# Resorting two turns of a fused linear-attention and SSM kernel: where projections, loads and scans stand

## Chip, core and metric

The kernel runs on one core of one Trainium2 chip. The metric is device time in microseconds (us), a median of runs. The core has a matrix engine (TensorE, PE, whose weight loads are listed apart as PEld), a vector engine (VectorE, DVE), an activation engine (ScalarE, ACT), a general engine (GpSimd, POOL) and a queue engine (SyncE, SP) that issues DMAs. Each engine works through its own list of instructions in order, and waits on semaphores for the others. The order of these lists is written by hand in this kernel, so the place of a call in the Python code is the place of its instructions on every engine.

## What is computed

Gated linear attention over 4 batches, 8 heads, 768 positions and 48 channels, then an SSM block over the heads laid side by side (384 channels):

```python
for t in range(S):                      # attention
    state = alpha[:, :, t, :, None] * state + einsum('bhd,bhde', k[:, :, t], v[:, :, t])
    y[:, :, t] = einsum('bhd,bhde->bhe', q[:, :, t], state)
x = y.transpose(0, 2, 1, 3).reshape(B, S, H * D)
proj = x @ w_in                         # 384 -> 2 * 512
val, gate = proj[..., :512], proj[..., 512:]
for t in range(S):                      # SSM
    h = exp(A_log)[0] * h + val[:, t]
    ys[:, t] = h
out = (silu(gate) * ys) @ w_out         # 512 -> 384
```

All data is float32. The inputs q, k, v and alpha have the shape (4, 8, 768, 48).

## The kernel before

The sequence is cut into 12 groups of 256 positions (`N`), three for each batch, and each group into two chunks of 128. The attention of a group is done by chunks, with running products of alpha, and the SSM of a group follows one turn later. In turn `n` of the main loop (L1012) the kernel does the SSM of group `n`, the attention of group `m = n + 1`, and the running products of group `n + 2`. The diff touches turns 1 to 3, the second to the fourth of the twelve when group 0's SSM ahead of the loop is counted as the first. They have code of their own (n < 3 at L1028, n == 3 at L1069); from turn 4 on the turns are alike.

The pieces of a turn, with the lines that the profile names:

- `products(m)` (L656) is a generator that works on DVE alone but for one check on ACT (`check_alpha`, L631). Its seven steps are: (1) turn alpha by a transposition (L660), put start values in place (L671, L672); (2) the forward scan of products (L674); (3) the ratio and reciprocal (L681 or L683, L687) and the reverse scan of inverse products (L695); (4) turn k into the tile Z (L660); (5) multiply it by the inverse products (L704); (6) turn q into Z (L660); (7) multiply it by the products (L704). `go(count)` lets it do that many steps; a `go` with more than is left does what is left.
- `keys(m, c)` (L717 on PE, L718 on ACT) turns k's half of Z into position-major form.
- `scores(m, c)` (L727) multiplies keys and queries. `masks` makes the result causal: the near half on DVE (L754), the far half by a copy on ACT (L742) and a multiplication on POOL (L743). `masks_apart`, used from turn 3 on, does both halves by ACT (L749) and POOL (L750).
- `state` (L786, L789), `values` (L765) and `carried` (L776) give the attention's output y in PSUM.
- `join(m, engines)` (L791) copies y to SBUF on ACT (L795, L796) and moves it by eight small DMAs (L812) into xT, the SSM's input, with channels on partitions; two heads go by ACT directly (L802). `engines[s]` issues the four moves of the half `s` of the heads.
- `block(n, cc)` (L845) is one quarter of the projection: `project` (L827) multiplies the value half and the gate half, each three matmuls of 256 columns, which the profile shows as six records; `hidden` (L835) is the SSM's scan on DVE; `gate` is Silu on ACT (L842) and a multiplication into the tile f on POOL (L843). `output(n)` (L856, L864, L865) multiplies f by w_out, and stores the result.

`mm` hands out three PSUM banks in a ring, one to each half of a block, to each `keys` and to each half of an output. A half can start once the engine that read the bank's previous tenant is done: DVE's scan for a value half, ACT's Silu for a gate half.

Loads go through SP. `loads(m)` issues alpha, k and q of a group (four DMAs each), `load_v` two for v. `ahead()` (L1022) issues `loads(n + 3)` and `load_v(n + 2)`. Up to eight of SP's DMAs are under way: each issue waits until the eighth before it has landed.

Of the kernel before, what the change touches and what calls it, by code (L numbers as in the profile page):

```python
# [351 lines left out]
def fast(  # L352
# [21 lines left out]
    nc = tc.nc  # L374
# [32 lines left out]
    def pair_of(*dims, dtype=FP32, which=None):  # L407
        if next(next_pair) if which is None else which:
            return [end_ps.tile([C, *dims], dtype, tag=f"b{b}", name="pair") for b in (4, 5)]
        t = both()  # L410
        n = dims[0] * dims[1]
        return [t[:, i, 0:n].rearrange("p (x y) -> p x y", x=dims[0]).bitcast(dtype) for i in range(2)]
# [8 lines left out]
    def load_raw(name, m, engines):  # L421


        b, g = divmod(m, NG)
        src = {"a": alpha, "q": q, "k": k}[name]
        t = raw_bufs[m % NR][name]
        n = 0
        for i in range(2):
            for odd in range(2):
                engines[n % len(engines)].dma_start(  # L430
                    out=t[ds(64 * i + 32 * odd, 32), :, 0:NT * D - 32 * odd],
                    in_=src[b, i::2, ds(g * GC, GC), :]
                    .rearrange("h (c j) d -> c h (j d)", c=32)[:, :, 32 * odd:])
                n += 1
# [16 lines left out]
    def load_v(m, engine, cs=range(G)):  # L451
        b, g = divmod(m, NG)
        for c in cs:
            engine.dma_start(out=vs[m % NV][:, c, :, 0:D],
                             in_=v[b, :, ds(g * GC + c * C, C), :].rearrange("h p d -> p h d"))
# [151 lines left out]
    def natural_qk(m, name, c, tp):  # L607

        if m not in Zs:
            Zs[m] = p2.tile([C, 4, 2, GC], FP32, tag="Z", name="Z")  # L610
        turned(name, m, c, tp)

        def times():
            i, by = {"k": (1, invs), "q": (0, prods)}[name]
            cols = ds(c * C, C)
            if m < 1:
                by = (inv_c[c][:, 1:] if name == "k" else prod_c[c]).rearrange("p (h n) -> p h n", h=4)
            else:
                by = by[:, :, cols]
            nc.vector.tensor_mul(Zs[m][:, :, i, cols], tp, by)  # L620
        return times
# [89 lines left out]
    def keys(m, c, b=None):  # L711

        if (m % NG) * G + c == NG * G - 1:
            return
        tp = mm(4, C, b=b)
        for p in range(4):
            nc.tensor.transpose(tp[:, p, :], Zs[m][:, p, 1, ds(c * C, C)], ident)  # L717
        nc.scalar.activation(ktms[c].rearrange("p a i d -> p a (i d)"), tp, AF.Copy)  # L718
# [11 lines left out]
    def masks(m, c, near_first=False):  # L730
        if near_first:
            masks_near(m, c)
        masks_far(m, c)
        if not near_first:
            masks_near(m, c)
# [55 lines left out]
    def join(m, engines, later=False):  # L791

        y = ys.pop(m)
        y_sb = p2.tile([C, 4, GC], FP32, tag="y_sb", name="y_sb")
        nc.scalar.activation(y_sb[:, 1::2], y[1], AF.Copy)  # L795
        nc.scalar.activation(y_sb[:, 2], y[0][:, 1], AF.Copy)  # L796
        xT = xTs[m] = p2.tile([C, NK, GC], FP32, tag="xT", name="xT")

        def in_place():
            for h in (0, 4):  # L800
                kk, row = divmod(h * D, C)
                nc.scalar.activation(xT[ds(row, D), kk], y[0][ds(16 * h, D), 0], AF.Copy)  # L802

        if not later:
            in_place()
        for h in (1, 5, 3, 7, 2, 6):
            s, a = divmod(h, 4)
            d = 0
            while d < D:
                kk, row = divmod(h * D + d, C)  # L810
                size = min(D - d, C - row)
                engines[s].dma_start(out=xT[ds(row, size), kk], in_=y_sb[ds(64 * s + d, size), a])  # L812
                d += size
        return in_place
# [5 lines left out]
    def project(n, cc):  # L820
        if cc == 0:
            fs[n] = end_sb.tile([C, NI, GC], FP32, tag="f", name="f")
        xT = xTs[n]
        pv, pg = mm(GC), mm(GC)
        for vg, pj in enumerate((pv, pg)):
            for kk in range(NK):
                nc.tensor.matmul(pj, w_in[cc][vg][:, kk, :], xT[:, kk, :],  # L827
                                 start=(kk == 0), stop=(kk == NK - 1))
        return pv, pg
# [3 lines left out]
    def hidden(n, cc, pv):  # L833
        hh = p2.tile([C, GC], FP32, tag=f"h{cc}", name="hh")
        nc.vector.tensor_tensor_scan(  # L835
            out=hh, data0=a_dec[:, cc:cc + 1].to_broadcast([C, GC]), data1=pv,
            initial=prev_h[cc][:, GC - 1:GC] if n % NG else 0.0, op0=ALU.mult, op1=ALU.add)
        prev_h[cc] = hhs[n, cc] = hh

    def gate(n, cc, pg):  # L840
        sg = p2.tile([C, GC], FP32, tag="sg", name="sg")
        nc.scalar.activation(sg, pg, AF.Silu)  # L842
        return lambda: nc.gpsimd.tensor_mul(fs[n][:, cc, :], sg, hhs.pop((n, cc)))  # L843

    def block(n, cc):  # L845
        pv, pg = project(n, cc)
        hidden(n, cc, pv)
        gate(n, cc, pg)()
# [24 lines left out]
    SP, ACT = nc.sync, nc.scalar  # L873

    def loads(m):
        for name in "akq":
            load_raw(name, m, [SP])
# [134 lines left out]
    for n in range(1, N):  # L1012
        m = n + 1
        att = m < N
        steps = products(n + 2) if n + 2 < N else iter(())

        def go(count):
            for _ in range(count):
                next(steps, None)


        def ahead():  # L1022
            if n + 3 < N:
                loads(n + 3)
            if n + 2 < N:
                load_v(n + 2, SP)

        if n < 3:  # L1028
            if n == 1:
                block(n, 0)  # L1030
                for times in [natural_qk(m, name, c, tp) for c in range(G)
                              for name, tp in zip("kq", pair_of(4, C))]:
                    times()
                block(n, 1)
            ahead()
            for c in range(G):
                keys(m, c)
            for c in range(G):
                scores(m, c)
            go(1)  # L1040
            for c in range(G):
                masks(m, c)
            if n == 2:
                block(n, 0)
                go(1)
                block(n, 1)
                go(1)
            else:
                block(n, 2)
                go(1)  # L1050
            state(m, 0)
            values(m, 0)
            values(m, 1)
            state(m, 1)
            carried(m, 0)
            carried(m, 1)
            join(m, (nc.gpsimd, nc.gpsimd) if m == 2 else (SP, SP))
            if n == 2:
                go(2)
                block(n, 2)  # L1060
            go(1)
            block(n, 3)
            go(10)
            output(n)()
            continue

        if n == 3:  # L1069
            for c in range(G):  # L1070
                scores(m, c, 1 - c)
                masks_apart(m, c)
            for c in range(G):
                keys(m, c)
            ahead()
            go(4)
        else:
            state(n, 0)
            values(n, 0)
            values(n, 1)  # L1080
            state(n, 1)
            carried(n, 0)
            carried(n, 1)
            in_place = join(n, (SP, nc.gpsimd), later=True)
            if att:
                scores(m, 0, 1)
                masks_apart(m, 0)
                in_place()
                scores(m, 1, sc=[mm(4, C, b=b) for b in "01"])
                masks_apart(m, 1)  # L1090
                keys(m, 0, "6")
                keys(m, 1, "4")
            else:
                in_place()
            next_mm = itertools.cycle("160")
            ahead()
            go(4)
            output(n - 1, "50")()
        for cc in range(NI):
            block(n, cc)  # L1100
            go(1)
            if cc == 0 and n == N - 1:
                next(end, None)
            if cc == 2 and n > 3:
                for _ in itertools.islice(checks, 2):
                    pass
        if n == N - 2:
            end = check_end()
            next(end)
# [61 lines left out]
```

## Time and profile before

| what | value |
|---|---|
| median of 3 runs | 291.07 us (291.03 to 291.84) |
| the profiled execution | 291.08 us, of which the span from the first to the last instruction is 289.3 us |
| granted TensorE clock | 1.000 |
| DMA | 42.08 MB in 70734 packets, 47508 of them under 512 bytes |
| turns 4 to 10 | about 21.9 us each, from one first projection to the next on PE (118.77, 140.68, 162.61, ...) |
| turns 1, 2, 3 on PE | turn 1 from 47.18 to 70.87, turn 2 to 93.90, turn 3 to 107.27, where turn 4 begins |

A line of the page's list gives an engine's busy time, its share of the span and its instructions. A line of the timeline gives start and length in us, engine, source line, operation, output and inputs, shape and count; in brackets stands how long the engine was idle before it, and what released it. Matmuls overlap in PE's pipeline and their ends are modelled, so that a length is a little more than the time until the next start. In the view of one tile, a line gives the shortest, median and longest duration in ns, and the first and last start in us. "To landing" is the time from a DMA's issue to its last byte.

### The profile page before, as it was taken

Reading aid. Unit: us, or ns where it says so; the run is one execution under the profiler, and the core shown is the slowest. Engines: PE = TensorE matmul, PEld = TensorE weight load, DVE = VectorE, ACT = ScalarE, POOL = GpSimd, SP = SyncE. Lnnn points to the kernel's source line nnn. Section 1 sums busy time; section 2 is a strip of 40 time slices with the busy share of each in tenths; the row PEclk is TensorE's granted clock in tenths of the full one; section 3 lists DMA queues with packets and bytes.
Section 4 is the critical chain, followed back from the end, with each engine's and each line's share of the span. In section 5 each row is a group of like instructions: output and inputs, shape, how many; then the busy total and the mean of one; then the engine's idle time right before and its main releaser. Section 6 shows DMA issues by size and latency. Waiting matters only on the chain. (4 is left out here: it accounts for less than half of the span.)

```text
span 289.3 us, 6236 instructions
## 1 busy us (share of the span) xinstructions
PE 279.4 (97%) x2353; PEld 227.2 (79%) x2353; DVE 211.2 (73%) x263; ACT 109.1 (38%) x242; POOL 139.2 (48%) x165
## 2 busy tenths in 40 slices
PE   7699999999999999999999999999999999999985
PEld 6478877885886988788788788788788788687874
DVE  5998896999999999399599599599589580131221
ACT  2447634432441626316316415416416415313110
POOL 7147792375532765526725725625734734633130
PEclk9999999999999999999999999999999999999999
DMA  9999969999997992992991991991892400201101
GB/s 130 163 162 299 376 129 185 173 250 211 231 220 106 221 200 53 215 205 54 228 189 43 217 204 42 206 212 48 191 198 77 113 2 25 73 0 30 69 5 61
DMA packets 70734, 42.08 MB, mean 145 GB/s; under 512 B 47508, under 2 KB 69656, under 8 KB 70696
## 3 DMA queue, kind: packets, MB, share of 16 engines
q1 hardware_dynamic: 68240, 39.78, 69.8%
q0 software_dynamic: 1408, 1.62, 2.3%
q8 instruction: 20, 0.33, 0.5%
q10 hardware_dynamic: 1048, 0.20, 0.4%
q14 instruction: 18, 0.15, 0.2%
HBM read 33.33 MB, written 4.72 MB: 131 GB/s over the span
## 5 line engine op out<-in xcount | busy, mean ns | idle before, releaser
L827 PE MATMUL mm<-xT,w_in 128*128 128x256 f32 x576 | 127.7, 380 | 0.3 <-ACT A L742 0.3
L827 PEld LDWEIGHTS mm<-xT,w_in 128*128 128x128 f32 x576 | 108.7, 190 | 17.7 <-issue 0.6
L843 POOL TENSOR_TENSOR f<-sg,hh 128x256 f32<-128x256 f32 x48 | 40.4, 843 | 87.2 <-ACT sg L842 61.8
L835 DVE TENSOR_TENSOR_SCAN hh<-a_dec,hh,mm 128x256 f32<-128x256 f32 x32 | 23.7, 741 | 49.6 <-PE mm L827 44.9
L856 PE MATMUL mm<-w_out,f 128*128 128x384 f32 x176 | 59.4, 489 | 0.1
L842 ACT ACTIVATE sg<-mm 128x256 f32<-128x256 f32 x48 | 18.5, 385 | 98.7 <-PE mm L827 96.6
L750 POOL TENSOR_TENSOR A<-A,mask 128x512 f32<-128x512 f32 x32 | 47.7, 1519 | 5.5 <-ACT A L749 5.4
L856 PEld LDWEIGHTS mm<-w_out,f 128*128 128x128 f32 x176 | 32.5, 190 | 21.4 <-POOL f L843 1.0
L812 POOL DMA_DIRECT2D xT<-y_sb x44 | 22.7, 521 | 28.4 <-ACT y_sb L796 26.8
L674 DVE TENSOR_TENSOR_SCAN prod<-aT,first 128x1024 f32<-128x1024 f32 x10 | 23.4, 2340 | 0.3
L695 DVE TENSOR_TENSOR_SCAN inv<-aT,last 128x1025 f32<-128x1025 f32 x10 | 22.9, 2294 | 0.3
L765 PE MATMUL pair<-A,v 128*64 128x128 f32 x352 | 21.3, 274 | 0.0
L864 ACT ACTIVATE o_sb<-mm 128x384 f32<-128x384 f32 x22 | 10.8, 491 | 25.4 <-PE mm L856 25.2
L727 PE MATMUL pair<-Z 48*128 48x128 f32 x272 | 18.9, 282 | 0.8 <-DVE first L640 0.3
L727 PEld LDWEIGHTS pair<-Z 48*128 48x128 f32 x272 | 16.4, 187 | 3.7 <-issue 2.1
L765 PEld LDWEIGHTS pair<-A,v 128*64 128x64 f32 x352 | 19.1, 137 | 0.0
L743 POOL TENSOR_TENSOR A<-A,mask 128x512 f32<-128x512 f32 x8 | 10.1, 1274 | 17.9 <-ACT A L742 17.9
L660 DVE STREAM_TRANSPOSE Z<-raw_k 128x1024 f32<-128x1024 f32 x9 | 18.4, 2047 | 0.0
L660 DVE STREAM_TRANSPOSE aT<-raw_a 128x1024 f32<-128x1024 f32 x9 | 18.4, 2046 | 0.0
L660 DVE STREAM_TRANSPOSE Z<-raw_q 128x1024 f32<-128x1024 f32 x9 | 18.2, 2024 | 0.0
L835 DVE TENSOR_TENSOR_SCAN hh<-a_dec,mm 128x256 f32<-128x256 f32 x16 | 10.8, 676 | 8.6 <-PE mm L827 7.0
L786 PEld LDWEIGHTS st<-v,ktm 128*64 128x64 f32 x320 | 11.4, 137 | 3.5 <-issue 3.5
(128 smaller groups left out, 300.7 us busy)
## 6 DMA issues: line engine op xcount, KB each, us to landing
raw_k<-in_k_dram SPq DMA_DIRECT2D x24, 192.0 KB, 5.3
raw_q<-in_q_dram SPq DMA_DIRECT2D x24, 192.0 KB, 6.6
v<-in_v_dram SPq DMA_DIRECT2D x24, 192.0 KB, 7.1
raw_a<-in_alpha_dram SPq DMA_DIRECT2D x23, 192.0 KB, 4.0
out_dram<-o_sb SPq DMA_DIRECT2D x22, 192.0 KB, 4.0
raw_a<-in_alpha_dram SPq DMA_DIRECT2D x18, 176.0 KB, 4.5
raw_k<-in_k_dram SPq DMA_DIRECT2D x18, 176.0 KB, 5.5
raw_q<-in_q_dram SPq DMA_DIRECT2D x18, 176.0 KB, 7.0
```

Source lines behind the costliest of these rows:

```text
L660: nc.vector.transpose(out=to.rearrange("p h (c j) -> p h j c", j=NT), in_=raw_bufs[m % NR][name].rearrange("p h (j d) -> p h j d", d=D)[:, ...
L674: nc.vector.tensor_tensor_scan(out=prod, data0=al, data1=first.rearrange("p h n -> p (h n)"), initial=0.0, op0=ALU.mult, op1=ALU.max)
L695: nc.vector.tensor_tensor_scan(out=inv[:, ::-1], data0=aT[:, ::-1], data1=lasts[:, 0:4 * GC + 1][:, ::-1], initial=0.0, op0=ALU.mult, op1= ...
L727: nc.tensor.matmul(sc[i][:, p, :], Z[rows, p, 1, cols], Z[rows, p, 0, cols], start=True, stop=True)
L750: nc.gpsimd.tensor_mul(A[:, i], A[:, i], mask_all())
L765: nc.tensor.matmul(ys[m][i][ds(64 * s, 64), e, ds(c * C, C)], v_sb[:, c, 2 * p + i, :], A[:, i, p, :], start=(c == 0 and e == 0), stop=Fal ...
L812: engines[s].dma_start(out=xT[ds(row, size), kk], in_=y_sb[ds(64 * s + d, size), a])
L827: nc.tensor.matmul(pj, w_in[cc][vg][:, kk, :], xT[:, kk, :], start=(kk == 0), stop=(kk == NK - 1))
L835: nc.vector.tensor_tensor_scan(out=hh, data0=a_dec[:, cc:cc + 1].to_broadcast([C, GC]), data1=pv, initial=prev_h[cc][:, GC - 1:GC] if n % ...
L842: nc.scalar.activation(sg, pg, AF.Silu)
L843: return lambda: nc.gpsimd.tensor_mul(fs[n][:, cc, :], sg, hhs.pop((n, cc)))
L856: nc.tensor.matmul(os[c], fs[n][:, cc, ds(c * C, C)], w_out[:, cc, :], start=(cc == 0), stop=(cc == NI - 1))
```

## The change

Three places change, and no instruction is added or dropped.

In turn 1 only alpha of group 4 is loaded at the old place. Its k and q, and v of group 3, are loaded behind `join`, whose moves are now issued half by SP and half by POOL instead of by POOL alone.

In turn 2 the projection's first block comes ahead of `keys`; blocks 1 and 2 follow the masks, each with one step of the products behind it; the block that stood behind `join`, with two steps ahead of it, is gone from there. The steps of `products(4)` are taken in the same order, but the blocks' scans stand elsewhere between them.

In turn 3 two instead of four steps of `products(5)` are taken before the blocks, one behind each block as before, and what is left behind the last. The last line, `go(10)`, stands in the code of all later turns too, where no steps are left by then.

```diff
             if n == 1:
                 block(n, 0)
                 ...
                 block(n, 1)
-            ahead()
+                load_raw("a", n + 3, [SP])
+            else:
+                ahead()
+                block(n, 0)
             for c in range(G):
                 keys(m, c)
             for c in range(G):
                 scores(m, c)
             go(1)
             for c in range(G):
                 masks(m, c)
             if n == 2:
-                block(n, 0)
-                go(1)
                 block(n, 1)
                 go(1)
-            else:
-                block(n, 2)
-                go(1)
+            block(n, 2)
+            go(1)
             state(m, 0)
             ...
             carried(m, 1)
-            join(m, (nc.gpsimd, nc.gpsimd) if m == 2 else (SP, SP))
-            if n == 2:
-                go(2)
-                block(n, 2)
+            join(m, (SP, nc.gpsimd) if m == 2 else (SP, SP))
+            if n == 1:
+                for name in "kq":
+                    load_raw(name, n + 3, [SP])
+                load_v(n + 2, SP)
             go(1)
             block(n, 3)
             go(10)
             output(n)()
             continue
         if n == 3:
             ...
             ahead()
-            go(4)
+            go(2)
         ...
         for cc in range(NI):
             block(n, cc)
             go(1)
             ...
+        go(10)
```

## The prediction

> **What bounds the kernel now.** I read the page first, then TensorE's (PE's) timeline, then the moves of y, then VectorE (DVE) beside GpSimd (POOL). Times are in us from the span's start.
>
> ```profile
> PE 279.4 (97%) x2353; PEld 227.2 (79%) x2353; DVE 211.2 (73%) x263; ACT 109.1 (38%) x242; POOL 139.2 (48%) x165
> ```
>
> PE is busy from about 24 to 281, so only PE's waits can be won and only new waits on PE can lose. Its timeline (start, length, line, what) around the edit:
>
> ```profile
> 65.49 5.54 PE L856 MATMUL mm<-w_out,f 128*128 128x384 f32 x16
> 70.87 1.04 PE L717 MATMUL mm<-ident,Z 128*128 128x128 f32 x8
> 72.19 2.06 PE L727 MATMUL pair<-Z 48*128 48x128 f32 x32 [0.28 <-DVE Z L704]
> 74.55 5.49 PE L827 MATMUL mm<-xT,w_in 128*128 128x256 f32 x24 [0.31 <-ACT A L742]
> 79.97 0.67 PE L786 MATMUL st<-v,ktm 128*64 128x48 f32 x16
> ...
> 93.90 2.06 PE L727 MATMUL pair<-Z 48*128 48x128 f32 x32
> 95.89 1.09 PE L717 MATMUL mm<-ident,Z 128*128 128x128 f32 x8
> 96.82 10.53 PE L827 MATMUL mm<-xT,w_in 128*128 128x256 f32 x48
> ...
> 113.59 5.34 PE L856 MATMUL mm<-w_out,f 128*128 128x384 f32 x16
> 118.77 10.52 PE L827 MATMUL mm<-xT,w_in 128*128 128x256 f32 x48
> 129.22 0.67 PE L786 MATMUL st<-v,ktm 128*64 128x48 f32 x16
> ```
>
> Ends are modelled, so I subtract starts and set each step beside its undisturbed twin. Output(1): 70.87-65.49 = 5.38 against 118.77-113.59 = 5.18, so 0.20 too long. Keys: 1.32 against 96.82-95.89 = 0.93, 0.39. Scores: 2.36 against 95.89-93.90 = 1.99, 0.37. Two blocks: 79.97-74.55 = 5.42 against half of 129.22-118.77 = 5.23, 0.19. Sum **1.15 us** lost in one place, the seam between the second and third turn; the rest of the span has no such seam except its start.
>
> The 0.31 is put down to an ACT copy that these matmuls don't read. The moves of y into xT say more (the xT tile from 63 to 75, the load of `a` that stands before it on SP, and the xT tile of the next turn, 85 to 94.5):
>
> ```profile
> L812 POOL DMA_DIRECT2D xT<-y_sb x8: 497/507/566, 63.8 to 67.4; - x8
> DMA to landing us min/median/max: 6.9/7.9/8.1
> ```
>
> ```profile
> DMA to landing us min/median/max: 5.3/5.4/5.4
> ```
>
> ```profile
> L812 SPq DMA_DIRECT2D xT<-y_sb x8: 536/588/3705, 85.5 to 93.0; - x8
> DMA to landing us min/median/max: 1.8/2.0/6.3
> ```
>
> The last of eight moves is issued at 67.4 and lands 8.0 later, at 75.4: block(2,0) starts while its last rows are still coming. So y's moves end the wait, behind loads that fill the DMA engines.
>
> DVE and POOL block each other:
>
> ```profile
> 58.89 2.80 DVE L674 TENSOR_TENSOR_SCAN prod<-aT,first 128x1024 f32<-128x1024 f32 x1
> 61.72 0.52 DVE L683 TENSOR_SCALAR ratio<-prod 128x4 f32<-128x4 f32 x1
> ```
>
> ```profile
> 57.04 2.50 POOL L743 TENSOR_TENSOR A<-A,mask 128x512 f32<-128x512 f32 x2 [1.47 <-ACT A L742]
> 60.04 2.17 POOL L843 TENSOR_TENSOR f<-sg,hh 128x256 f32<-128x256 f32 x1 [0.50 <-DMA raw_q<-in_q_dram]
> ```
>
> ```profile
> 99.50 2.25 DVE L704 TENSOR_TENSOR Z<-Z,inv 128x1024 f32<-128x1024 f32 x1
> 101.67 0.67 DVE L835 TENSOR_TENSOR_SCAN hh<-a_dec,mm 128x256 f32<-128x256 f32 x1
> ```
>
> The scan (2.29 elsewhere) begins inside a mask that ends at 59.54 and takes 0.5 more; f (0.73) begins inside the scan and ends 0.52 after it. The multiplication (1.2) is held by a mask in the same way. The hidden scan L835, 0.6 to 0.75 everywhere, is not.
>
> [...] POOL's moves land 6.9 to 8.1 after issue, about when SP's loads of the same moment do, as in one line. I go by the measurement.
>
> **The change, part by part.**
>
> *Turn n=1, loads and moves.* Four of y's moves go to SP, four stay on POOL; k and q of group 4 (8 issues) and v of group 3 (2) follow them on SP instead of preceding them. SP's last issue of `a` stays at 61.6 and lands at 61.6+5.4 = 67.1. y_sb is ready at 63.8; both queues then issue four moves at 0.5 to 0.6 each, done by 66.1. In the line stand only `a` and the eight moves. Estimate for a move's share: in before, eight loads and eight moves landed from 67.1 to 75.7; a load takes about 0.8 (landings of `a`), so a move (8.6-6.4)/8 = 0.28. The last lands at 67.1+8x0.28 = 69.3. DMA never empties, so k, q and v land about when they did (v about 77.5, wanted at 81.6) and SP arrives at turn 2's loads about as before. POOL has four issues fewer: f(1,3) starts at 66.2 rather than 67.9, and output(1) no longer waits (the 0.20).
>
> *Turn n=2, PE.* block(2,0) starts at 70.65, 1.3 after its data, and covers what keys and scores waited for (Z's q by 72.0). Then keys 0.95, scores 2.0, blocks 1 and 2 at 5.3: state at 81.6. Block 2 has left the place after the join; what follows is unchanged (3.4, block 2.65, output 5.25). Scores(4) can start at 92.85, before 93.90. One switch between kinds of matmul more costs an estimated 0.1: 1.15-0.10 = **1.05 gained**.
>
> *Turn n=2, DVE and POOL.* DVE order: hidden, turn of `a` (2.04), near masks, hidden, scan, hidden, inverse scan, turn of k, hidden, and then three rather than one of Z's steps (1.2, 2.0, 1.2). POOL's far masks now follow ACT's check of alpha [...], so the scan ends at 81.5 rather than 80.8; inverse scan to 85.1, k turned 87.1, hidden 87.7, Z done at 92.1. Slack 0.75 before scores(4): no stall. xT(3): its first issue still waits behind v's loads (3.7 before), last issue about 93.1, landed about 95; wanted from 95.8. No stall, slack 0.8.
>
> *Turn n=3.* Here it costs. Before, `go(4)` put both long scans and k's turn ahead of the blocks; now the inverse scan stands between hidden(3,0) and hidden(3,1). DVE: turn of `a` 92.0, scan 94.4 to 96.65. POOL's four masks arrive from 94.7. Mask 1 waits for the scan, ends 97.75; hidden(3,0) 97.3 to 97.9 (block(3,0) at 95.8 plus 1.5); mask 2 is already running, to 98.95; [...] mask 3 to 100.2; then the inverse scan, 100.2+2.15 = 102.35; hidden(3,1) to **102.95**. The gate half of block(3,2) reuses the bank of value half (3,1): with three banks in a ring and two taken by a block, that is its second successor. PE wants it at 95.77+2x2.61+1.31 = 102.3. It gets it at about 103.0: **0.7 of new wait**, queued in front of all PE work. Before it was wanted at 96.82+6.53 = 103.35 and hidden(3,1) had ended at 101.67+0.67 = 102.34. Next: k turned 104.95, hidden(3,2) 105.55 against 105.6 wanted; Z(5) at 110.45 against 110.75. Just in time both.
>
> *Turn n=4.* DVE is 3.5 later than before but idles 4.3 ahead of hidden(4,0) at 120.3; the masks hold it to 122.25 against 122.35 wanted. The final `go(10)` finds steps left only at n=3. Nothing else moves.
>
> Sum: 1.05-0.7 = **0.35 gained, 0.3 taken** since three places have under 0.3 of slack. From 291.08 of the profiled execution (span 289.3) this is 290.8; the median, 291.07, is the same to 0.01.
>
> **Costs not shown before.** y's moves in a split pair at full DMA: from 1.9 after issue (idle DMA, next turn) to 8, taken 3.9. The wait at block(3,2): [...] 2 if one more mask (1.27) goes ahead; taken 0.7. A switch: 0 to 0.2.
>
> **Rivals.**
> 1. *Full gain.* The inverse scan does not wait for mask 3, so PE keeps 0.9 to 1.05: 290.1. For it: the order is decided by 0.2 us. [...] Chance 0.20.
> 2. *Likeliest, masks take most back*: 290.8 (290.3 to 291.5). Chance 0.62.
> 3. [...] One more mask before the inverse scan: hidden(3,1) at 104.2, PE at 104.3 instead of 103.35: 292.0. It decides once hidden(3,1) ends after 103.3. Chance 0.11.
> 4. *y's moves stay slow.* If they need 7.9 as before, issued till 65.9, block(2,0) starts at 73.8: 3.1 lost, 1.05 gained, the wait of turn 3 gone: 293. It decides from a landing after 71.7. Against: the line ahead of them is 5 us shorter. Chance 0.07.
>
> That the change doesn't do what it says is excluded by the instruction order: one block ahead of keys, six steps of DVE resorted.
>
> **How the numbers follow.** A measurement tells about 0.3% (0.87 us) from no change: faster means under 290.2, slower over 291.95. Rival 1 gives most of 0.19 for faster; rivals 3 and 4 give 0.17 for slower; 0.64 stay. The range, 290.0 to 291.9, leaves out the slow cases.
>
> **What would show it.** Right: in the new trace no gaps at keys, scores and block(2,0); xT(2) landed by 69.5; a step of some 0.7 in PE in the third block of turn 3, ended by DVE hh. Wrong: a gap at block(2,0), or scores(4) or scores(5) waiting for Z L704.

## The result, and the profile after

| | before | changed |
|---|---|---|
| median of 12 runs each | 291.75 us | 291.47 us |
| ratio of times, 95% interval | | 0.9998 (0.9982 to 1.0014) |
| profiled execution, its span | 291.08, 289.3 us | 290.68, 289.0 us |
| start of output(1) to turn 4's projection on PE | 53.28 us | 52.83 us |
| last matmul's start to the end of the span | 3.21 us | 3.80 us |

No change that the runs can tell. Single runs of the same kernel lie up to 1.8 us apart, so most of what follows is read from differences inside a trace. TensorE (PE) first, the changed kernel's timeline: start and length in us, line, operation, count, and in brackets the idle time ahead of it.

```profile
65.14 5.32 PE L856 MATMUL mm<-w_out,f 128*128 128x384 f32 x16
70.30 2.75 PE L827 MATMUL mm<-xT,w_in 128*128 128x256 f32 x12
72.89 1.04 PE L717 MATMUL mm<-ident,Z 128*128 128x128 f32 x8
73.86 2.06 PE L727 MATMUL pair<-Z 48*128 48x128 f32 x32
75.84 5.45 PE L827 MATMUL mm<-xT,w_in 128*128 128x256 f32 x24
81.22 0.67 PE L786 MATMUL st<-v,ktm 128*64 128x48 f32 x16
...
92.57 2.06 PE L727 MATMUL pair<-Z 48*128 48x128 f32 x32
94.55 1.09 PE L717 MATMUL mm<-ident,Z 128*128 128x128 f32 x8
95.48 6.64 PE L827 MATMUL mm<-xT,w_in 128*128 128x256 f32 x30
102.39 4.15 PE L827 MATMUL mm<-xT,w_in 128*128 128x256 f32 x18 [0.27 <-DVE hh L835]
106.47 0.67 PE L786 MATMUL st<-v,ktm 128*64 128x48 f32 x16
```

Every gap at the seam is gone: output(1) takes 70.30-65.14 = 5.16, keys 0.97, scores 1.98. From output(1) to scores(4), the end of turn 2, it is 92.57-65.14 = 27.43 against 93.90-65.49 = 28.41 before: 0.98 us won. In turn 3 a gap has opened inside the projection, ended by the hidden scan `hh`: from scores(4) to the state it is 106.47-92.57 = 13.90 against 107.27-93.90 = 13.37, so 0.53 us lost. Net 0.45 on PE.

Why the hidden scan is late stands in VectorE's (DVE) and GpSimd's (POOL) timelines of the changed kernel, 94 to 104:

```profile
96.98 0.69 DVE L835 TENSOR_TENSOR_SCAN hh<-a_dec,mm 128x256 f32<-128x256 f32 x1 [0.89 <-PE mm L827]
97.58 0.82 DVE L681 TENSOR_TENSOR ratio<-prod,last 128x4 f32<-128x4 f32 x1
98.44 0.18 DVE L687 RECIPROCAL last<-prod 128x4 f32<-128x4 f32 x1
98.66 3.10 DVE L695 TENSOR_TENSOR_SCAN inv<-aT,last 128x1025 f32<-128x1025 f32 x1
101.68 0.66 DVE L835 TENSOR_TENSOR_SCAN hh<-a_dec,mm 128x256 f32<-128x256 f32 x1
```

```profile
94.43 8.38 POOL L750 TENSOR_TENSOR A<-A,mask 128x512 f32<-128x512 f32 x4 [5.54 <-ACT A L749]
```

The ratio works on 4 numbers per partition and took 0.82 instead of 0.17, the reverse scan 3.10 instead of 2.29. Neither shows idle time before it: what holds them is found in their length, not in a gap. The four masks beside them took 8.38 instead of 7.11. hidden(3,1) ended at 102.34, and PE went on at 102.39.

y's moves, the xT tile of the changed kernel from 63 to 66:

```profile
L812 SPq DMA_DIRECT2D xT<-y_sb x4: 520/564/583, 63.2 to 65.1; - x4
L812 POOL DMA_DIRECT2D xT<-y_sb x4: 504/516/533, 63.5 to 65.0; - x4
...
DMA to landing us min/median/max: 4.1/4.3/4.5
```

All are issued by 65.1 and landed by about 69.5, 0.8 ahead of block(2,0) at 70.30.

The span sums up: output(1) starts 0.35 earlier (no instruction ahead of it differs, and other kernels below start it from 65.3 to 66.8), 0.45 are won in turns 1 to 3, turns 4 to 10 take 150.69 in both (first projection of turn 4 to that of turn 11), the last turn is 0.2 shorter up to its last matmul, and 0.6 are lost behind it. The last four matmuls of the changed kernel, and of the kernel before:

```profile
284.82 0.61 PE L1137 MATMUL o<-w_out,f 128*128 128x128 f32 x4
```

```profile
285.81 0.61 PE L1135 MATMUL o<-w_out,f 128*128 128x128 f32 x4
```

Their spans end at 288.96 and 289.35, so 4.14 and 3.54 us after the first of the four; counted from the last one's start, it is the 3.80 and 3.21 of the table. The experiments take up this end too.

### The profile page after: what moved, and what is told of

Same layout as the page of the kernel before. It is cut to its first block, busy times and chain, and to the rows that moved or that the text cites. A ratio compares the mean times of both kernels' runs of the same rounds, so it can differ in the third digit from the quotient of the medians.

```text
span 289.0 us, 6235 instructions
## 1 busy us (share of the span) xinstructions
PE 278.9 (97%) x2353; PEld 226.8 (78%) x2353; DVE 213.9 (74%) x263; ACT 109.0 (38%) x242; POOL 140.3 (49%) x161
## 5 line engine op out<-in xcount | busy, mean ns | idle before, releaser
L843 POOL TENSOR_TENSOR f<-sg,hh 128x256 f32<-128x256 f32 x48 | 39.6, 827 | 88.5 <-ACT sg L842 62.6
L750 POOL TENSOR_TENSOR A<-A,mask 128x512 f32<-128x512 f32 x32 | 51.7, 1643 | 5.6 <-ACT A L749 5.5
L812 POOL DMA_DIRECT2D xT<-y_sb x40 | 20.6, 520 | 28.5 <-ACT y_sb L796 28.5
L695 DVE TENSOR_TENSOR_SCAN inv<-aT,last 128x1025 f32<-128x1025 f32 x10 | 25.2, 2523 | 0.3
L674 DVE TENSOR_TENSOR_SCAN prod<-aT,first 128x1024 f32<-128x1024 f32 x10 | 24.0, 2396 | 0.3
L743 POOL TENSOR_TENSOR A<-A,mask 128x512 f32<-128x512 f32 x8 | 10.1, 1270 | 14.5 <-ACT A L742 14.5
```

Of the source, the lines that this page charges most:

```text
L674: nc.vector.tensor_tensor_scan(out=prod, data0=al, data1=first.rearrange("p h n -> p (h n)"), initial=0.0, op0=ALU.mult, op1=ALU.max)
L695: nc.vector.tensor_tensor_scan(out=inv[:, ::-1], data0=aT[:, ::-1], data1=lasts[:, 0:4 * GC + 1][:, ::-1], initial=0.0, op0=ALU.mult, op1= ...
L750: nc.gpsimd.tensor_mul(A[:, i], A[:, i], mask_all())
```

## The experiments

**The part of turn 1 alone.** Loads behind y's moves, moves split; turns 2 and 3 as before.

```diff
                 block(n, 1)
-            ahead()
+                load_raw("a", n + 3, [SP])
+            else:
+                ahead()
             ...
-            join(m, (nc.gpsimd, nc.gpsimd) if m == 2 else (SP, SP))
+            join(m, (SP, nc.gpsimd) if m == 2 else (SP, SP))
+            if n == 1:
+                for name in "kq":
+                    load_raw(name, n + 3, [SP])
+                load_v(n + 2, SP)
```

> Only the part of the change that concerns turn 1: k and q of group 4 and v of group 3 are loaded behind y's moves, and the moves go half by SP, half by POOL. Turns 2 and 3 stand as in the kernel before. My theory: the waits at the seam came from y's moves and from POOL's eight issues, so this part alone wins most of the 1.15 us there: output(1) takes 5.18, keys 0.95, scores at most 2.2, and from the start of output(1) to the start of scores(4) PE takes 27.4 to 27.6 us against 28.4 before (27.4 in the changed kernel). In turn 3 the reverse scan stays ahead of the blocks, so no wait at the third block: from scores(4) to the state of group 4 it takes 13.4 us as before (13.9 in the changed kernel). Net 0.9 us faster than before, ratio about 0.997, and about 0.5 us ahead of the changed kernel. Rival, that the projection block ahead of keys is what covers the waits: keys and scores keep 0.39 and 0.37 of wait, and at most 0.4 us is won.

Measured: ratio 0.9994 (0.9983 to 1.0005). Its PE timeline:

```profile
66.63 5.32 PE L856 MATMUL mm<-w_out,f 128*128 128x384 f32 x16
71.79 1.04 PE L717 MATMUL mm<-ident,Z 128*128 128x128 f32 x8
72.95 2.06 PE L727 MATMUL pair<-Z 48*128 48x128 f32 x32
74.93 5.45 PE L827 MATMUL mm<-xT,w_in 128*128 128x256 f32 x24
...
94.25 2.06 PE L727 MATMUL pair<-Z 48*128 48x128 f32 x32
96.23 1.09 PE L717 MATMUL mm<-ident,Z 128*128 128x128 f32 x8
97.16 10.53 PE L827 MATMUL mm<-xT,w_in 128*128 128x256 f32 x48
107.62 0.67 PE L786 MATMUL st<-v,ktm 128*64 128x48 f32 x16
```

94.25-66.63 = 27.62, so 0.79 of the changed kernel's 0.98 come from loads and moves alone; keys keep 0.23 of wait (1.16 against 0.93), and scores start at 72.95, as DVE ends its multiplication into Z (71.58 and 1.23 long). Turn 3 takes 107.62-94.25 = 13.37 with no gap. On PE this part beats the whole change by 0.35 us. The ratio of 0.997 that I expected was missed: from the last matmul to the end it takes 3.80, as in the changed kernel.

**The resorting alone.** Turn 1 as before, turns 2 and 3 as in the changed kernel.

```diff
-                load_raw("a", n + 3, [SP])
-            else:
-                ahead()
+            ahead()
+            if n == 2:
                 block(n, 0)
             ...
-            join(m, (SP, nc.gpsimd) if m == 2 else (SP, SP))
-            if n == 1:
-                ...
+            join(m, (nc.gpsimd, nc.gpsimd) if m == 2 else (SP, SP))
```

> The resorted turns 2 and 3 as in the changed kernel, but turn 1 as before: all loads of group 4 and v of group 3 ahead of y's moves, all eight moves from POOL. My theory (moves and loads land as in one line): the last move lands about 75.0 as before, but block(2,0) now wants it at 70.5, so PE stands still for 3.5 to 4.5 us ahead of it or inside it. The wait at the third block of turn 3 is gone, since PE is later than DVE there. Net 2.5 to 3.5 us slower than before, ratio 1.009 to 1.012. Rival ([...] the long landing is POOL's own): the moves' landing doesn't matter to this order and block(2,0) starts within 1 us of 70.7; ratio 1.000 to 1.003.

Measured: ratio 1.0147 (1.0118 to 1.0176). In its PE timeline and its xT tile (64 to 76):

```profile
66.30 5.54 PE L856 MATMUL mm<-w_out,f 128*128 128x384 f32 x16
74.64 2.83 PE L827 MATMUL mm<-xT,w_in 128*128 128x256 f32 x12 [2.80 <-issue]
...
106.81 4.15 PE L827 MATMUL mm<-xT,w_in 128*128 128x256 f32 x18 [0.27 <-DVE hh L835]
```

```profile
L812 POOL DMA_DIRECT2D xT<-y_sb x8: 497/507/566, 64.6 to 68.2; - x8
DMA to landing us min/median/max: 6.4/7.2/7.4
```

The last move is issued at 68.2 and lands about 75.2; PE stands 2.80 at block(2,0), although the timeline can name no releaser ("issue"). The moves' lateness that cost 0.3 to 0.5 in the old order costs 2.8 in the new one: the block ahead of keys needs moves that land early. The wait came out below the 3.5 to 4.5 that I gave, the ratio above the 1.009 to 1.012: two runs lie in that range, two 1.2 us above it (see the clock, below).

One more thing was missed. The wait of turn 3 was to vanish, since PE is later here. It stayed: from scores(4) at 96.98 to the state at 110.89 it is 13.91, and `hh` ends the gap. DVE's forward scan of turn 3 is as late against PE as in the changed kernel: it ends 3.5 us after the start of scores(4) in both (100.51-96.98 and 96.09-92.57), and only 0.5 after it in the kernel before (94.39-93.90). So the resorting brings this wait by itself.

**The old go(4) in turn 3.**

```diff
             ahead()
-            go(2)
+            go(4)
```

> The changed kernel with the old go(4) in turn 3: the reverse scan and k's turn stand ahead of the blocks again. My theory ([...] the reverse scan comes after two masks wherever it stands): the scan ends at about 100.6, k is turned by 102.6, hidden(3,0) ends at about 103.1, and the gate half of the second block, which reuses its bank, waits from 99.4 to 103.2: 3.8 us instead of the 0.53 at the third block. About 3 us slower than the changed kernel, ratio to before 1.008 to 1.011. Rival (the reverse scan's place between the blocks is itself the loss): the wait goes away and it is 0.5 us faster than the changed kernel, ratio 0.997.

Measured: ratio 1.0178 (1.0154 to 1.0202). PE's timeline, and PE in three stretches (length, PE busy, granted clock, DMA):

```profile
97.11 4.05 PE L827 MATMUL mm<-xT,w_in 128*128 128x256 f32 x18
104.63 9.59 PE L827 MATMUL mm<-xT,w_in 128*128 128x256 f32 x30 [3.47 <-DVE hh L835]
114.15 0.67 PE L786 MATMUL st<-v,ktm 128*64 128x48 f32 x16
```

```profile
97.00:101.00 4.00, 4.00 (x21) 1.00 0.98 261
104.60:110.40 5.80, 5.77 (x14) 0.50 1.22 198
110.40:114.00 3.60, 3.60 (x18) 1.00 0.16 19
```

The new order of turn 3 is no needless loss: with the new turn 2, the old order puts the wait one block earlier and makes it 3.6 us, near the 3.8 expected. But the time is some 5.2 us above the kernel before, where 2.3 to 3.2 were expected. After the idle stretch the clock is granted at 0.50 for 5.8 us of work, and records start 0.427 apart instead of 0.216, which costs about 3 us more. The profiled run is the slowest of the four (298.32 us, mean clock 0.988); the others, at 296.14 to 296.97 with 0.994, lost less.

**No masks on POOL in turn 3.** Group 4's scores are left unmasked.

```diff
             nc.scalar.activation(A[:, i], sc[i], AF.Copy)
-            nc.gpsimd.tensor_mul(A[:, i], A[:, i], mask_all())
+            if m != 4:
+                nc.gpsimd.tensor_mul(A[:, i], A[:, i], mask_all())
```

> The changed kernel without POOL's four multiplications of group 4's scores by the mask in turn 3 (left out: the causal mask of that group; its scores stay full). My theory [...]: the ratio takes 0.15 instead of 0.82 and the reverse scan 2.29 instead of 3.10, hidden(3,1) ends by 101.0 and PE no longer waits at the third block; from scores(4) to the state of group 4 13.37 us instead of 13.90. Net 0.5 us less than the changed kernel, ratio to before about 0.997. Rival (the order on DVE alone makes the wait, whatever POOL does): hidden(3,1) still ends after 102 and 13.9 us stay.

Measured: ratio 0.9982 (0.9972 to 0.9992). Its DVE timeline from 97 and its PE timeline:

```profile
97.75 0.14 DVE L681 TENSOR_TENSOR ratio<-prod,last 128x4 f32<-128x4 f32 x1
97.92 0.18 DVE L687 RECIPROCAL last<-prod 128x4 f32<-128x4 f32 x1
98.14 2.29 DVE L695 TENSOR_TENSOR_SCAN inv<-aT,last 128x1025 f32<-128x1025 f32 x1
100.35 0.66 DVE L836 TENSOR_TENSOR_SCAN hh<-a_dec,mm 128x256 f32<-128x256 f32 x1
```

```profile
92.73 2.06 PE L727 MATMUL pair<-Z 48*128 48x128 f32 x32
...
95.65 10.53 PE L828 MATMUL mm<-xT,w_in 128*128 128x256 f32 x48
106.11 0.67 PE L787 MATMUL st<-v,ktm 128*64 128x48 f32 x16
```

Ratio and scan are short again, hidden(3,1) ends 8.28 us after the start of scores(4) instead of 9.77, and PE has no gap: 13.38. So the masks on POOL make the 0.53; the order on DVE alone makes no wait. The masks alone don't either: the part of turn 1 alone has them, with turns 2 and 3 as before, and takes 13.37. The ratio is short of the 0.997 expected; the end takes 3.80 here too.

**Group 3's moves split as well.** To test the end of the kernel: with this, SP issues as many DMAs as before the change. First on the part of turn 1 alone, then on the whole change.

```diff
-            join(m, (SP, nc.gpsimd) if m == 2 else (SP, SP))
+            join(m, (SP, nc.gpsimd))
```

> The part of turn 1 alone (loads behind y's moves, moves half by SP, half by POOL), and group 3's moves split in the same way, so that SP issues as many DMAs in all as before. Seen so far: every kernel that issues four more DMAs on SP takes 3.80 us from its last matmul to the end of the span, the two others 3.2. Theory: SP's DMAs go round eight semaphores, four more shift the last output's place in the round, and the waits for all eight that close the kernel then have less to hide behind. Here the end takes 3.2 us again, the seam 27.6 us and turn 3 13.4 us as with the part of turn 1 alone: 0.8 us on PE and nothing lost at the end, ratio 0.997 to 0.9975. Rival (the end's 0.6 us has another cause, or the measured 0.06% is all that there is to win): the end stays at 3.8, ratio 0.999 to 1.0.

Measured: ratio 0.9980 (0.9970 to 0.9990). The end takes 3.21, the seam 27.62 and turn 3 13.37 in its trace. This is the lowest ratio of a kernel that computes everything: 0.6 us, and clear of no change, though short of the 0.997 to 0.9975 expected.

> The changed kernel with group 3's moves split between SP and POOL, so that SP issues as many DMAs as in the kernel before. Theory of the round of eight semaphores: the end takes 3.2 us instead of 3.8; the wait at the third block of turn 3 stays at 0.5; from output(1) to turn 4's projection 52.8 us as in the changed kernel. 0.45 us on PE and nothing lost at the end: ratio 0.998 to 0.9985, behind the kernel with the part of turn 1 alone and the same split. Rival: end stays at 3.8, ratio 0.9998.

Measured: ratio 0.9984 (0.9972 to 0.9997). The end takes 3.32; turn 3 keeps its gap (0.28 idle, ended by `hh`), 52.84 from output(1) to turn 4. The interval excludes no change by little, and doesn't part this kernel from the one above, or from the changed kernel.

**The split alone.** Group 2's moves half by SP, half by POOL, all loads still ahead of them.

```diff
-            join(m, (nc.gpsimd, nc.gpsimd) if m == 2 else (SP, SP))
+            join(m, (SP, nc.gpsimd) if m == 2 else (SP, SP))
```

> The kernel before with group 2's moves split between SP and POOL, but all loads of turn 1 still ahead of them on SP. Theory (one line, and SP in order): SP's four moves stand behind k, q and v, and the first issue behind v is held some 4 us; they are issued from 70 to 76 and land about 78, where the first block wants them at about 73.5. PE waits 3 to 5 us at block(2,0); ratio 1.009 to 1.015. Rival (the split itself shortens the moves, the loads' place doesn't matter): block(2,0) starts without a wait, seam 27.6 us, ratio 0.998.

Measured: ratio 1.0215 (1.0195 to 1.0234). PE's timeline, and PE and the rest in a stretch ahead of and two behind the wait (length, then busy times of PE, PEld, DVE, ACT, POOL, granted clock, DMA):

```profile
71.93 2.06 PE L727 MATMUL pair<-Z 48*128 48x128 f32 x32
77.69 8.23 PE L827 MATMUL mm<-xT,w_in 128*128 128x256 f32 x24 [3.71 <-DMA xT<-y_sb]
```

```profile
72.00:77.00 5.00, 1.98 (x32) 1.79 (x32) 3.28 (x5) 2.67 (x6) 2.49 (x2) 0.96 0.98 140
77.70:83.50 5.80, 5.80 (x14) 4.63 (x15) 2.87 (x2) 0.25 (x1) 0.00 (x0) 0.51 0.98 238
83.50:88.00 4.50, 4.50 (x58) 3.94 (x58) 3.32 (x6) 0.85 (x3) 2.24 (x2) 1.00 1.09 210
```

Here the timeline names the moves. The split without the loads' new place is much worse than no split: SP's four moves stand behind k, q and v and are issued from 70.0 to 76.3 only. The wait is 3.7, and the clock adds some 3 (the two blocks take 8.17 us instead of 5.2); the ratio lies above the 1.009 to 1.015 expected. So the split needs the loads' new place. The other way round, that place with all moves from POOL, was not run.

**The kernel before with group 3's moves split.**

```diff
-            join(m, (nc.gpsimd, nc.gpsimd) if m == 2 else (SP, SP))
+            join(m, (nc.gpsimd, nc.gpsimd) if m == 2 else (SP, nc.gpsimd))
```

> The kernel before with nothing changed but group 3's moves split between SP and POOL: four DMAs fewer on SP. Theory of the round of eight semaphores: the place of the last output shifts by four as in the changed kernel, and the end takes 3.8 us instead of 3.2 while PE's work up to the last matmul is as long as before (53.3 us from output(1) to turn 4's projection): 0.6 us slower, ratio 1.002. Rival (the 0.6 us of the end belongs to turn 1's loads and moves): end 3.2, ratio 1.000.

Measured: ratio 1.0011 (1.0000 to 1.0022); the end takes 3.45, and 53.02 stand from output(1) to turn 4. The direction is as expected, the size is 0.24 instead of 0.6. With the last outputs on other semaphores of the round, SP passes four waits more behind the landing of the last; in the changed kernel one of these waits takes 0.4 (287.4 to 287.8), although nothing lands any more, and here, with an end of 3.45, it does not. What that 0.4 is stays open.

The end follows the number of DMAs on SP in all ten traces: 3.80 us in the five kernels with 240, 3.20 to 3.32 in the four with 236, as many as before the change, and 3.45 in this one, with 232. As 232 and 240 differ by a full round of eight, the place in the round is the same, and accounts for 0.24 of the 0.6 only.

This trace also shows how well the seam is known: its code there is that of the kernel before, and output(1) to scores(4) takes 28.16 instead of 28.41. With the loads' new place it repeats to 0.01: 27.62 in two traces without the resorting, 27.42 to 27.43 in four with it.

## Why the prediction was right, point by point

*The seam.* 1.05 was predicted for PE up to scores(4), 0.98 measured (0.73 against the other trace of the old seam). The 0.10 taken off for one more switch between kinds of matmul was an estimate; in the trace before, the twelve matmuls of a single block take 2.59 to 2.79 up to the start of the next kind (47.18 to 49.77, 56.62 to 59.41), so that 0 to 0.2 is what it shows. The landing of y's moves was put at 69.3 and came by about 69.5 in a trace that runs 0.35 ahead; moves and loads go as in one line, as the resorting alone and the split alone show from two sides. In the resorting alone, a move that POOL issued at 64.64 lands at 71.00, between loads that SP issued at 64.33 and 65.02 and that land at 70.72 and 71.62. The time to landing goes with what is ahead: a median of 7.2 us behind all loads (resorting alone) and 4.3 behind fewer (changed kernel).

*What earns it.* This step was read too generously for the block: it "covers what keys and scores waited for", but 0.79 of the 0.98 come without it, because y's moves and POOL's four issues fewer were behind most of the seam. The resorting adds 0.19 and brings the wait of turn 3.

*Turn 3.* 0.7 of new wait was predicted at the gate half of the third block, ended by hidden(3,1); it is there, with 0.53. Masks and scan came in the predicted order, and the run without masks shows that they are the cause. In the changed kernel the ratio, 0.82 instead of 0.17, begins inside the second mask (97.12 to 98.34) and ends at 98.40; the reverse scan begins inside the third (98.34 to 99.57) and ends at 101.76, 2.2 behind it; the fourth takes 3.25 and ends at 102.82. So the traces show that the two engines hold each other up, not by what.

*Just in time.* Scores(4), scores(5) and the second block of turn 4 were put at 0.1 to 0.75 of slack; none of them waits. The slack of 0.8 for y's moves of group 3 was not there: the last is issued at 93.7 and lands at 95.7, after block(3,0) began at 95.48. No gap shows.

*The sum.* 0.35 was worked out for PE, 0.45 is in the trace; the seam came out 0.07 smaller and the new wait 0.17 smaller than predicted. That it isn't seen in the runs has a cause that no step had. "Nothing else moves" was wrong: with SP's four further DMAs, 0.6 us are lost behind the last matmul, more than the 0.45 that PE wins. With as many DMAs on SP as before, the change is at 0.9984. The median, 291.47, lies in the range, but 0.7 above the 290.8 of the likeliest case, as the kernel before came out at 291.75 in twelve runs and not at 291.07. And the forecast of no change tests the steps little: 0.35 won and 0.6 lost unforeseen both lie under the 0.87 us that the prediction takes as the least that a measurement tells. The trace is what bears the steps out.

*The rivals.* "One more mask" and "full gain" did not come, nor did late moves in the changed kernel. The price of late moves, 293, was too low: the resorting alone, where they come late, takes 294.65 to 296.16. The wait of turn 3 does not go away with them, and the clock can add to a wait: about 3 us behind 3.5, at 0.50 granted (old go(4)).

## What to carry to other kernels

Before a block is moved to cover a wait, ask what ends that wait: here putting the loads behind the moves, with the moves split, earned most of it, and no block had to move. Where an engine's instruction grows long without a gap ahead of it, look for what another engine does at that time: here the ratio took 0.82 instead of 0.17 beside POOL's masks, and 0.14 without them. When a gain of PE does not arrive in the time, look behind the last matmul, where even the number of DMAs of a queue can tell (3.80 us with 240 on SP, 3.20 to 3.32 with 236).

## What the runs showed of the hardware that was not expected

In two runs a wait of PE cost nearly twice its length. After 3.5 and 3.7 us of idle time (old go(4), split alone) the granted clock was 0.50 and 0.51 over the next 5.8 us, which costs about 3 us more in each; after 2.80 us (resorting alone, profiled) it was 1.00 over the next 5.4 us, and the records went on 0.216 us apart.

The length of the wait is not all that decides. PE's clock within the long wait of the old go(4), whose last matmul ends at 101.16 (two stretches, in the columns of its table above):

```profile
101.20:103.50 2.30, 0.00 (x0) 1.00 1.10 211
103.70:104.60 0.90, 0.00 (x0) 0.50 1.08 216
```

It drops about 2.4 us after that end, and in the split alone about 2.6 us after it (0.50 from 76.6, last matmul to 73.98): sooner than the 2.80 that passed without a drop. As ends are modelled, here is the same from the last matmul's start: 2.8 and 2.9, against 3.3 without a drop. So the length of the idle time alone does not tell in these traces when the clock drops; what else counts is not shown.

The four runs of the resorting alone split in the same way: 294.65 and 294.89 us with a mean granted clock of 0.998 and 1.000, 296.10 and 296.16 with 0.994. The waits of the three runs that were only timed were not seen, so that the drop came in two of them is read from their mean clock and time alone; where in the run it came is not shown, and two of the 51 later runs of the kernel before have a mean of 0.994 too, at 291.53 and 292.34 us.
